# A fixed order for the first eight token tiles of a fused linear-attention and gated-MLP kernel

## The chip, the cores and the metric

The kernel runs on one core of one Trainium2 chip. A core has five engines that run their own instruction queues and meet only through semaphores: TensorE (PE, matrix products; PEld is its weight load), VectorE (DVE), ScalarE (ACT), GpSimd (POOL) and SyncE (SP), which here only issues DMA transfers. Sixteen DMA engines move data between HBM and the on-chip memory (SBUF). TensorE writes to PSUM, eight banks of 128 x 512 floats.

The metric is the device time of one execution in microseconds (us). A verdict compares the changed kernel with the kernel before on the same chip.

## The reference

```python
xn = layernorm(x)                              # x: 1 x 2048 x 1024, no gain or bias, eps 1e-5
q, k, v = heads(xn @ wqkv)                     # 32 heads of 32
phi(u)  = [softmax(u @ w_phi), softmax(-u @ w_phi)]
kv, z   = phi(k)^T v, sum over tokens of phi(k)
s = merge(phi(q) kv / (phi(q) z + 1e-6)) @ wo
h = sigmoid(xn @ w_gate) * (xn @ w_up)         # 1024 -> 3584
out = x + s * silu(h @ w_down)
```

All in 32-bit floats.

## The kernel before, in words

The 2048 tokens are two chunks of 1024, a chunk is eight tiles of 128 tokens. The large products (V, K and Q projections, gate and up, down, output) are each done as seven products of half-size blocks instead of eight (a Strassen-like scheme). The seven operand pairs are called B11, T2, T3, B21, T1, T4 and B22. Each operand needs sums of input blocks on the activation side and sums of weight blocks on the weight side. A float32 product is made of three matmuls of a reduced 32-bit type: `split` writes a high part (ScalarE cast, L124) and a low part (VectorE subtraction, L125), and `mm3` (L127 to L131) multiplies high by high, high by low and low by high into one bank.

The opening of chunk 0 is what concerns us. For each of its eight tiles: the tile is loaded (L151), VectorE takes mean and variance (L161, L162), a chain of nine small operations makes scale and shift (L166 to L175, on GpSimd for chunk 0, with one square root on ScalarE and one reciprocal on VectorE), ScalarE normalizes the tile in place (L177), TensorE transposes it in two halves of four blocks (L193), and ScalarE copies the halves out of PSUM (L197). Tiles 0 to 3 give the blocks B11 and B21, which are also split straight from PSUM; tiles 4 to 7 give B12 and B22. With the matching tile of the first four they form the sums T1, T3, T2 and T4 in `x_sums` (L201 to L207): T1 = B12 - B11 on GpSimd, T3 = B22 - B12 on VectorE, T2 = B22 - T1 on VectorE, T4 = B21 - T2 on GpSimd. T3 and T2 overwrite B12 in a ring of two half slots.

Meanwhile the V projection runs: its products in the order B11, B21, T2, T3, T4, T1, B22, each with four groups (one per 128 tokens) of twelve matmuls. Its weight operands are prepared by `prep` (L334), which splits two of four weight rows at a time into a ring of eight slots; the loop calls it as often as slots are free. Four sums of the raw weight blocks of v, two on VectorE and two on GpSimd, are made in `v_sums` (L248 to L255, two halves each) and stored for the second chunk. The K and Q weights are first multiplied with w_phi in `fold`: a load of wqkT, TensorE matmuls with block-diagonal head blocks `bd` (L278), copies (L279), sums on GpSimd (L227 to L230) and stores (L280). The head blocks are filled by GpSimd in `phi_blocks` (L733). A queue called `side` holds the opening's steps; one step is taken after each group of a projection product: tile 1, tiles 2 and 3 with the head blocks, tiles 4 and 5, v's sums, tiles 6 and 7, four K folds, the rest of the operands (`x_rest`), four Q folds.

The order of the instructions on each engine's queue is not that of the program. A planner places them by priority (program order) and by its own timeline of costs, within the data dependencies; `issue_after` and `high_priority` nudge it. Each queue then runs strictly in its order: an instruction that waits holds up all behind it. Before the first tile arrives, TensorE does 28 warm-up transposes of an identity (L719).

Of the kernel before, what the change touches and what calls it, by code (L numbers as in the profile page):

```python
# [48 lines left out]
def hedgehog_glu_kernel(  # L49
# [54 lines left out]
    WARM = 28  # L104
# [43 lines left out]
    last_norm, last_chain = [], []  # L148
# [5 lines left out]
    def norm(tiles, xs):  # L154
        n = len(tiles)
        st = small.tile([P, 2, 2, 6], F32, name=f"bn{tiles[0]}", tag="bn")
        mv = small.tile([P, 2, 2], F32, name=f"mv{tiles[0]}", tag="mv")
        ws = small.tile([P, 4, 2], F32, name=f"lnw{tiles[0]}", tag="lnw")
        for i, xt in enumerate(xs):
            for a in range(2):  # L160
                nc.vector.bn_stats(st[:, i, a], xt[:, a * HB:(a + 1) * HB])  # L161
            nc.vector.bn_aggr(mv[:, :, i], st[:, i])  # L162
        v, r, a, b = [ws[:, q, :n] for q in range(4)]

        eng = nc.gpsimd if tiles[0] < CTT else nc.vector
# [9 lines left out]
        last_chain[:] = [eng.tensor_scalar(b, b, -1.0, None, op0=ALU.mult).ins]  # L175
        for i, xt in enumerate(xs):
            last_norm[:] = [nc.scalar.activation(xt, xt, AF.Identity, bias=b[:, i:i + 1], scale=r[:, i:i + 1]).ins]  # L177
# [9 lines left out]
    def transpose(t, xt, dst):  # L187

        c, th, u = t // CTT, t % CTT // 4, t % 4
        for q in range(2):  # L190
# [6 lines left out]
            nc.scalar.copy(dst[q], tp)  # L197
            if c and i is not None:
                operand(c, i, u, dst[q])

    def x_sums(c, u, first, second):  # L201
        (b11, b21), (b12, b22) = first, second
        t2 = b22 if c else b12
        for i, o, a, b in ((T1, b11, b12, b11), (T3, b12, b22, b12), (T2, t2, b22, b11), (T4, b21, b21, t2)):
            (nc.vector if c == 0 and i in (T2, T3) else nc.gpsimd).tensor_sub(o, a, b)
            if c or i in (T2, T3):
                operand(c, i, u, o)  # L207
# [39 lines left out]

    def v_sums():  # L248
        vec, pool = nc.vector.tensor_tensor, nc.gpsimd.tensor_tensor
        for f, o, a, b, op in ((vec, 3, 2, 3, "add"), (vec, 2, 0, 2, "subtract"),  # L250
                               (pool, 0, 3, 0, "subtract"), (pool, 1, 1, 0, "subtract")):
            for h in range(2):
                f(whole(VA[o] + h), whole(VA[a] + h), whole(VA[b] + h), op=getattr(ALU, op))
# [42 lines left out]
    flow = dict(item=0, made=0, used=0)  # L296
# [36 lines left out]
    def prep():  # L333
        if flow["item"] == len(items):  # L334
            return False
# [168 lines left out]
    def x_task(t):  # L504
        xt = x_load(t, 52)
        norm([t], [xt])
        th, u = t % CTT // 4, t % 4
        transpose(t, xt, halves(53 + th))
# [547 lines left out]
```

## Time and profile before

| what | value |
|---|---|
| median of three runs | 2437.62 us (2436.7 to 2439.03) |
| the profiled execution's own time | 2438.41 us |
| its span, first to last instruction | 2436.6 us |
| TensorE matmul busy | 2389.2 us, 98% |
| VectorE, ScalarE, GpSimd busy | 1717.3, 1006.8, 989.3 us |
| HBM traffic over the span | 245 GB/s |

A row of a group of instructions gives the line, the engine, the operation, what it writes and reads, the shape, how many there are, then the busy time in us with the mean of one in ns, and after the second bar the idle time of the engine just before them with what ended it. A row of the timeline gives start and duration in us. A row of the windows gives for each engine the busy time and in brackets the number of instructions, then the clock granted to TensorE (1.00 is full), the share of time that the DMA engines were busy, and what they moved in GB/s. A row of the waits gives who waited for whom: us in total, times, the longest. K stands for the K projection, which follows V.

### The profile page before, as it was taken

The numbers are of one execution on the slowest core, as the hardware profiler recorded it, in microseconds if no ns is written. First come the engines' busy times: TensorE is split into PE (matmuls) and PEld (weight loads), VectorE is DVE, ScalarE is ACT, GpSimd is POOL, SyncE is SP. The second block draws the span as 40 slices with busy tenths as digits, with TensorE's granted clock in tenths as the row PEclk, the third lists the DMA queues.
The fourth block names the chain that finished last, engine by engine and source line by source line (L and its number), as shares of the span: only waits on it lengthen the run. The fifth ranks groups of instructions, "written<-read, shape, count | busy, mean of one in ns | idle before, by whom it ended". The sixth has DMA issues, their size and how long they took to land.

```text
span 2436.6 us, 32010 instructions
## 1 busy us (share of the span) xinstructions
PE 2389.2 (98%) x11076; PEld 1984.5 (81%) x11076; DVE 1717.3 (70%) x2247; ACT 1006.8 (41%) x1499; POOL 989.3 (41%) x665
## 2 busy tenths in 40 slices
PE   7999999999999999999999999999999999999998
PEld 6788778888888878888888888888888888888887
DVE  6535577778777679747867888646888988855454
ACT  6432344444444344314444444423443334453332
POOL 5540255756656442222353222323333335414554
PEclk8999999999999999999999999999999999999999
DMA  7887787767777787777777666587666666867554
GB/s 275 271 300 248 255 299 259 271 248 268 260 261 249 255 293 249 265 263 250 261 267 272 221 215 224 191 288 247 221 233 238 217 209 229 286 233 251 173 178 147
DMA packets 233234, 599.44 MB, mean 246 GB/s; under 512 B 30576, under 2 KB 30576, under 8 KB 228464
## 3 DMA queue, kind: packets, MB, share of 16 engines
q1 hardware_dynamic: 233072, 597.40, 71.8%
q8 instruction: 87, 1.43, 0.2%
q14 instruction: 75, 0.61, 0.1%
HBM read 361.10 MB, written 236.19 MB: 245 GB/s over the span
## 4 chain that ended last, share of the span: by engine, by line
PE 74%; DMA 7%; DVE 7%; issue 5%; POOL 4%; ACT 2%; SPq 0%; ACTq 0%; POOLq 0%; DVEq 0%
PE bank L129 24%; PE bank L131 24%; PE bank L130 24%; DMA wo_d<-fc 3%; DVE w L125 1%; PE bank L458 1%; DVE x L125 1%; PE bank L630 1%; DVE p L125 1%; DMA fb<-wqkT 1%; DMA fc<-xo_d 1%; PE bank L278 0%; DVE fc L125 0%; DMA out<-fc 0%; DMA fc<-wo 0%
## 5 line engine op out<-in xcount | busy, mean ns | idle before, releaser
L129 PE MATMUL bank<-x,w 128*128 128x512 f32 x2352 | 912.8, 390 | 8.0 <-ACT fb L837 2.3
L130 PE MATMUL bank<-x,w 128*128 128x512 f32 x2352 | 915.7, 389 | 0.0
L131 PE MATMUL bank<-x,w 128*128 128x512 f32 x2352 | 907.1, 389 | 0.0
L129 PEld LDWEIGHTS bank<-x,w 128*128 128x128 f32 x2352 | 441.5, 188 | 102.9 <-ACT fb L837 2.7
L131 PEld LDWEIGHTS bank<-x,w 128*128 128x128 f32 x2352 | 441.6, 188 | 92.0 <-DVE w L125 0.4
L124 ACT CAST w<-fa 128x512 fp32r<-128x512 f32 (+1 forms) x444 | 307.6, 697 | 504.7 <-PE bank L130 371.0
L130 PEld LDWEIGHTS bank<-x,w 128*128 128x128 f32 x2352 | 441.7, 188 | 90.2 <-DVE x L125 0.3
L125 DVE TENSOR_TENSOR w<-fa,w 128x512 fp32r<-128x512 f32 (+1 forms) x444 | 438.5, 992 | 108.7 <-ACT w L124 101.6
L129 PE MATMUL bank<-w,x 128*128 128x512 f32 x708 | 279.5, 395 | 7.8 <-DVE fc L388 3.2
L131 PE MATMUL bank<-w,x 128*128 128x512 f32 x708 | 277.8, 393 | 1.8 <-DVE x L125 1.8
L130 PE MATMUL bank<-w,x 128*128 128x512 f32 x708 | 277.3, 392 | 0.0
L847 POOL TENSOR_TENSOR fb<-fb,fc 128x512 f32<-128x512 f32 x57 | 88.9, 1560 | 243.3 <-DVE fc L846 218.2
L129 PEld LDWEIGHTS bank<-w,x 128*128 128x128 f32 x708 | 133.8, 189 | 38.9 <-DVE fc L388 3.4
L131 PEld LDWEIGHTS bank<-w,x 128*128 128x128 f32 x708 | 133.5, 189 | 29.8 <-DVE x L125 2.5
L130 PEld LDWEIGHTS bank<-w,x 128*128 128x128 f32 x708 | 133.9, 189 | 26.8
L587 POOL TENSOR_TENSOR fc<-fc 128x1024 f32<-128x1024 f32 x32 | 81.5, 2548 | 182.0 <-ACT fc L423 127.5
L846 DVE TENSOR_TENSOR fc<-fc,bank 128x512 f32<-128x512 f32 x84 | 57.4, 684 | 103.7 <-PE bank L131 92.8
L125 DVE TENSOR_TENSOR x<-fa,x 128x512 fp32r<-128x512 f32 x112 | 114.7, 1024 | 18.0 <-ACT x L124 17.9
L125 DVE TENSOR_TENSOR w<-fb,w 128x512 fp32r<-128x512 f32 (+1 forms) x114 | 102.4, 899 | 32.8 <-ACT w L124 31.1
L124 ACT CAST w<-fb 128x512 fp32r<-128x512 f32 (+1 forms) x114 | 71.3, 626 | 118.7 <-PE bank L130 97.0
L599 POOL TENSOR_TENSOR fc<-fc,sa 128x1024 f32<-128x1024 f32 x32 | 70.4, 2199 | 101.1 <-DVE sa L596 101.1
L847 POOL TENSOR_TENSOR fc<-fc 128x512 f32<-128x512 f32 x27 | 43.4, 1608 | 134.8 <-DVE fc L846 106.9
(246 smaller groups left out, 3281.1 us busy)
## 6 DMA issues: line engine op xcount, KB each, us to landing
ws_d<-w SPq DMA_DIRECT2D x112, 512.0 KB, 4.2
w<-ws_d SPq DMA_DIRECT2D x112, 512.0 KB, 5.0
fa<-w_gu SPq DMA_DIRECT2D x84, 512.0 KB, 4.2
fa<-h_d SPq DMA_DIRECT2D x84, 512.0 KB, 4.3
fa<-wf_d SPq DMA_DIRECT2D x32, 1024.0 KB, 6.3
h_d<-fc SPq DMA_DIRECT2D x120, 256.0 KB, 3.6
fc<-e_d SPq DMA_DIRECT2D x48, 512.0 KB, 3.7
fc<-qkv_d SPq DMA_DIRECT2D x80, 256.0 KB, 4.7
```

The lines of the kernel that those rows point to most:

```text
L124: nc.scalar.copy(o[0], src)
L125: return nc.vector.tensor_sub(o[1], src, o[0].bitcast(F32))
L129: nc.tensor.matmul(o, a[0], b[0], start=first, stop=False, **kw)
L130: nc.tensor.matmul(o, a[0], b[1], start=False, stop=False, **kw)
L131: nc.tensor.matmul(o, a[1], b[0], start=False, stop=last, **kw)
L458: nc.tensor.matmul(kvb[g // 2][:, g % 2 * 256:g % 2 * 256 + 256], v[:, g].rearrange("p a f -> p (a f)"), ph[:, g].rearrange("p a f -> p (a ...
L587: nc.gpsimd.tensor_mul(ez, e, zb)
L599: nc.gpsimd.tensor_mul(e3, e3, r2[:, :, None].to_broadcast([P, 32, DH]))
L630: nc.tensor.transpose(ps[:, j * P:(j + 1) * P], e[:, k * P:(k + 1) * P], ident)
L846: v = nc.vector.tensor_add(b, u2 if q == 3 else u1, bank)
L847: nc.gpsimd.tensor_mul(g, g, b)
```

## The change

The eight tiles of chunk 0 get an order written out by hand. A context manager `in_order` adds, for all instructions traced inside it, an order without a wait between each one and the one traced before it on the same engine. The opening becomes a generator `tiles()` of nine steps; each step is traced in order on VectorE, ScalarE and GpSimd. The first step runs before the V loop, the others from `side`. From the start until after the fourth group of the first product, TensorE's instructions are ordered too.

Besides: 36 warm-up transposes instead of 28; tile 1 is loaded before v's first weight block, which is loaded in two halves; the scale chain of tiles 0 to 3 runs on VectorE (tiles 2 and 3 share one), that of tiles 4 to 7 stays on GpSimd; the copies of tiles 0 to 3 out of PSUM are put off and done two at a time (`keep_two`); `prep` is held to one weight item per `made()` until the ninth step; T2 is now made as T3 + B11, T3 and T2 are written to slots of their own, B12 gets four half slots; T1 and T4 follow on GpSimd at the end; three of v's four weight sums are on VectorE and they come in the sixth step; the head blocks are filled in the fifth. The loads of tiles 6 and 7 and v's last two weight blocks stand in the first and second steps. The K folds start four steps of `side` later than before.

```diff
-    WARM = 28
+    WARM = 36
...
+    @contextmanager
+    def in_order(*engines):
+        traced = nc.cur_bb.bb.instructions
+        last = traced[-1]
+        yield
+        start = next(k for k in reversed(range(len(traced))) if traced[k] is last) + 1
+        for i in traced[start:]:
+            if i.engine in engines:
+                if i.engine in queued:
+                    tc.add_manual_dep(i, queued[i.engine].name,
+                                      mybir.DependencyInfo(mybir.DependencyClass.NoSync, mybir.DependencyReason.DATA),
+                                      reason="in_order")
+                queued[i.engine] = i
...
-        eng = nc.gpsimd if tiles[0] < CTT else nc.vector
+    def scales(tiles, mv, eng=nc.vector):
...
-    def transpose(t, xt, dst):
+    def transpose(t, xt, dst, kept=None):
...
                 operand(c, i, u, tp)
-            nc.scalar.copy(dst[q], tp)
+                kept.append((dst[q], tp))
+            else:
+                nc.scalar.copy(dst[q], tp)
...
+            yield
...
     def v_sums():
...
+        v_sum(nc.vector, 3, 2, 3, "add")
+        v_sum(nc.vector, 2, 0, 2, "subtract")
+        v_sum(nc.vector, 0, 3, 0, "subtract")
+        v_sum(nc.gpsimd, 1, 1, 0, "subtract")
...
-        if flow["item"] == len(items):
+        if flow["item"] == min(len(items), flow["until"]):
             return False
...
-    b12s, b22s = Ring(halves(10)), halves(8, 9)
+    b12s, b22s = halves(10, 26), halves(8, 9)
+    t3s, t2s = halves(52, 53), halves(27, 24)
...
-    v_load(0)
-    xts += [x_load(t, XS[t]) for t in range(1, 4)]
+    xts.append(x_load(1, XS[1]))
+    for h in range(2):
+        nc.sync.dma_start(slots[39 + h], v_block(0, 0)[:, 2 * h:2 * h + 2])
+    xts += [x_load(t, XS[t]) for t in range(2, 4)]
...
+    def t32(u):
+        nc.vector.tensor_sub(t3s[u], b22s[u], b12s[u])
+        nc.vector.tensor_add(t2s[u], t3s[u], first[u][0])
+        operand(0, T2, u, t2s[u])
+
+    def t14():
+        for u in range(4):
+            (b11, b21), b12 = first[u], b12s[u]
+            nc.gpsimd.tensor_sub(b11, b12, b11)
+            nc.gpsimd.tensor_sub(b21, b21, t2s[u])
+
+    def tiles():
+        for n in range(WARM):
+            nc.tensor.transpose(banks[3][:, n % 4 * P:(n % 4 + 1) * P], ident, ident)
+        mv0, take = stats((0,))
+        take(0, xts[0])
+        normalized(xts[0], *scales((0,), mv0))
+        mv1, take = stats((1,))
+        take(0, xts[1])
+        rb = scales((1,), mv1)
+        parts = transpose(0, xts[0], first[0], kept)
+        made()
+        next(parts)
+        made()
+        next(parts)
+        normalized(xts[1], *rb)
+        xts.append(x_load(6, XS[6]))
+        yield
+        parts = transpose(1, xts[1], first[1], kept)
+        mv, take = stats((2, 3))
+        next(parts)
+        take(0, xts[2])
+        keep_two()
+        next(parts)
+        take(1, xts[3])
+        rb = scales((2, 3), mv)
+        normalized(xts[2], *rb, 0)
+        xts.append(x_load(7, XS[7]))
+        v_load(2)
+        v_load(3)
+        yield
+        parts = transpose(2, xts[2], first[2], kept)
+        next(parts)
+        keep_two()
+        next(parts)
+        normalized(xts[3], *rb, 1)
+        mv, take = stats((4, 5))
+        take(0, xts[4])
+        made()
+        yield
+        parts = transpose(3, xts[3], first[3], kept)
+        next(parts)
+        keep_two()
+        next(parts)
+        take(1, xts[5])
+        rb = scales((4, 5), mv, nc.gpsimd)
+        made()
+        normalized(xts[4], *rb, 0)
+        keep_two()
+        yield
+        mv, take = stats((6, 7))
+        take(0, xts[6])
+        second(4)
+        normalized(xts[5], *rb, 1)
+        t32(0)
+        take(1, xts[7])
+        rb = scales((6, 7), mv, nc.gpsimd)
+        phi_blocks()
+        yield
+        second(5)
+        v_sums()
+        normalized(xts[6], *rb, 0)
+        t32(1)
+        yield
+        second(6)
+        normalized(xts[7], *rb, 1)
+        made()
+        t32(2)
+        yield
+        second(7)
+        made()
+        t32(3)
+        yield
+        for u in range(4):
+            operand(0, T3, u, t3s[u])
+            if u % 2:
+                made()
+        t14()
+        flow["until"] = len(items)
+        yield
...
-    todo(x_tiles, 1)
-    todo(lambda: (x_tiles(2, 3), phi_blocks()))
-    todo(x_tiles, 4, 5)
-    todo(v_sums)
-    todo(x_tiles, 6, 7)
+    first_products = in_order(PE)
+    first_products.__enter__()
+    in_turn()
+    for _ in range(3):
+        todo(in_turn)
+    todo(first_products.__exit__, None, None, None)
+    for _ in range(5):
+        todo(in_turn)
```

97 lines of the change are left out of this document (49 added, 48 removed).

## The prediction

> **What bounds the kernel now.** I read the page's engine totals first, then the opening in windows, the waits of TensorE up to 130 us, and the groups and timelines that price single instructions.
>
> ```profile
> PE 2389.2 (98%) x11076; PEld 1984.5 (81%) x11076; DVE 1717.3 (70%) x2247; ACT 1006.8 (41%) x1499; POOL 989.3 (41%) x665
> ```
> TensorE is the bound. The change touches only the part before K's products, so the question is how much TensorE time is lost there, and where. Windows (busy us, instructions in brackets, granted clock, DMA share and GB/s):
> ```profile
> 5.10:8.51 3.41, 1.39 (x13) 1.15 (x11) 1.24 (x4) 0.20 (x1) 1.28 (x7) 1.00 1.04 410
> 18.75:22.17 3.42, 0.76 (x4) 0.30 (x3) 3.28 (x7) 1.34 (x3) 2.04 (x5) 1.00 1.05 387
> 22.17:25.58 3.41, 3.41 (x12) 3.05 (x13) 1.69 (x5) 2.23 (x5) 2.59 (x10) 0.50 1.07 395
> 47.20:59.30 12.10, 7.26 (x38) 6.40 (x36) 8.79 (x10) 10.36 (x18) 4.83 (x4) 0.72 0.34 120
> 59.30:78.00 18.70, 18.70 (x118) 16.68 (x119) 17.23 (x17) 9.75 (x17) 15.47 (x10) 1.00 0.71 220
> 78.00:146.40 68.40, 64.28 (x362) 54.62 (x362) 27.62 (x33) 24.84 (x39) 33.63 (x26) 1.00 0.94 314
> ```
> The hole is at 47 to 59 us; from 59 on TensorE has work, and from 78 the DMA engines are nearly full too (0.94). The waits of TensorE up to 130 us name the holes:
> ```profile
> PE bank L193 <- ACT x L177: 6.2, 2, 3.5
> PE bank L193 <- ACT x L197: 3.6, 1, 3.6
> ```
> Transposes waited twice for normalized tiles (3.5 us for tile 0, the rest for tile 1) and once for a bank (tiles 6 and 7). How much TensorE had done by two instants, in groups up to 34.66 us and then up to 59.2 us:
> ```profile
> L129 PE MATMUL bank<-w,x 128*128 128x512 f32 x16 | 7.9, 496 | 0.4 <-ACT x L124 0.4
> L131 PE MATMUL bank<-w,x 128*128 128x512 f32 x16 | 7.4, 462 | 1.8 <-DVE x L125 1.8
> L130 PE MATMUL bank<-w,x 128*128 128x512 f32 x16 | 7.2, 449 | 0.0
> L193 PE MATMUL bank<-ident,x 128*128 128x128 f32 x32 | 5.8, 350 | 6.2 <-ACT x L177 6.2
> ```
> ```profile
> L129 PE MATMUL bank<-w,x 128*128 128x512 f32 x33 | 14.7, 444 | 0.7 <-ACT x L124 0.7
> L130 PE MATMUL bank<-w,x 128*128 128x512 f32 x33 | 13.8, 419 | 0.0
> L131 PE MATMUL bank<-w,x 128*128 128x512 f32 x32 | 13.5, 426 | 1.8 <-DVE x L125 1.8
> L193 PE MATMUL bank<-ident,x 128*128 128x128 f32 x48 | 9.5, 375 | 9.8 <-ACT x L177 6.2 <-ACT x L197 3.6
> L719 PE MATMUL bank<-ident 128*128 128x128 f32 x28 | 5.0, 361 | 1.5 <-POOL ident masks.py:199 1.5
> L193 PE MATMUL bank<-ident,fc 128*128 128x128 f32 x16 | 1.9, 272 | 0.0
> L278 PE MATMUL bank<-fb 128*128 128x128 f32 x8 | 1.9, 419 | 0.0
> L278 PE MATMUL bank<-fb,x 128*128 128x128 f32 x8 | 1.1, 278 | 0.0
> ```
> So 48 projection matmuls and 32 transposes by 34.66; 98, 64 and 16 fold matmuls by 59.2. At full clock a projection matmul starts every 0.23 us:
> ```profile
> 146.16 0.39 PE L131 MATMUL bank<-w,x 128*128 128x512 f32 x1
> 146.39 0.39 PE L129 MATMUL bank<-w,x 128*128 128x512 f32 x1
> ```
> A transpose or fold matmul is 0.12 (sixteen in 1.9). Work in 47.2 to 59.3 is 16 transposes, 16 folds and two matmuls, 4.1 us: that hole loses 8.0 us.
>
> **The change, part by part.** Prices, from ScalarE's and VectorE's timelines and groups:
> ```profile
> 8.70 1.24 ACT L177 ACTIVATE x<-x,lnw 128x1024 f32<-128x1024 f32 x1 [1.92 <-POOL lnw L175]
> 9.84 1.98 ACT L124 CAST w<-fa 128x1024 fp32r<-128x1024 f32 x2
> 11.72 1.06 ACT L124 CAST x<-bank 128x512 fp32r<-128x512 f32 x2
> ```
> ```profile
> 4.68 1.29 DVE L161 BATCH_NORM_STATS2 bn<-x 128x6 f32<-128x512 f32 x2 [4.68 <-DMA x<-x]
> 6.00 0.21 DVE L162 BATCH_NORM_AGGREGATE mv<-bn 128x2 f32<-128x12 f32 x1
> 6.80 0.16 DVE L168 RECIPROCAL lnw<-lnw 128x1 f32<-128x1 f32 x1 [0.59 <-ACT lnw L167]
> ```
> ```profile
> 379.19 0.16 DVE L171 TENSOR_TENSOR lnw<-lnw 128x1 f32<-128x1 f32 x1
> 379.38 0.15 DVE L172 TENSOR_SCALAR lnw<-lnw 128x1 f32<-128x1 f32 x1
> ```
> ```profile
> L125 DVE TENSOR_TENSOR x<-x,x 128x512 fp32r<-128x512 f32 x8 | 9.1, 1136 | 0.3
> L125 DVE TENSOR_TENSOR w<-fa,w 128x1024 fp32r<-128x1024 f32 x7 | 8.9, 1266 | 4.9 <-ACT w L124 4.7
> L161 DVE BATCH_NORM_STATS2 bn<-x 128x6 f32<-128x512 f32 x12 | 7.7, 679 | 7.6 <-DMA x<-x 7.6
> L125 DVE TENSOR_TENSOR x<-bank,x 128x512 fp32r<-128x512 f32 x8 | 5.3, 683 | 3.0 <-ACT x L124 3.0
> ```
> ```profile
> L253 DVE TENSOR_TENSOR p<-fb,p 128x1024 f32<-128x1024 f32 x2 | 2.4, 1263 | 0.0
> ```
> ```profile
> L253 POOL TENSOR_TENSOR fa<-p,fa 128x1024 f32<-128x1024 f32 x2 | 5.7, 2853 | 2.3 <-DVE fb L253 2.3
> ```
> ```profile
> L733 POOL COPY fb<-fc 32x256 f32<-32x256 f32 x4 | 1.6, 395 | 0.1
> ```
> In short: statistics 1.5 a tile, VectorE's scale chain 1.9 (seven links of 0.2, the square root and two hand-overs), normalizing 1.24, an x split 0.6 then 0.68, a weight split 1.0 then 1.2, a copy like an x cast, a v sum half 1.2.
>
> *To 34.7 us.* Eight more warm-up transposes run where TensorE waits anyway for tile 0: free; without that wait, 1 to 2 us. Tile 0's chain moves from GpSimd to VectorE: 4.7 + 1.5 + 1.9 = 8.1, normalized 9.3, 0.6 earlier. Tile 1 now loads ahead of v's first megabyte (one more DMA issue on SyncE's queue, no more bytes): at 410 GB/s it lands near 6.3. Its statistics and chain end at 11.4; the first weight split is done at 12.6, the x split at 13.3, the second weight split at 14.4, so product B11's first tile ends near 16.7, with six cold matmuls behind that split. Tile 1 is normalized by 14.3 and its transposes follow at once. But then the order blocks: tile 2's statistics stand behind tile 1's first split on VectorE: 16.6 + 0.4 + 0.6 + 0.7 = 18.6, then statistics, split, tile 3's statistics, chain, normalizing: 18.6 + 1.5 + 0.6 + 1.5 + 1.9 + 1.2 = 25.3. TensorE's second tile ends at 21.2, and B21 cannot fill the gap, for TensorE is ordered too until B11's fourth group: 4.1 us idle. Tile 3 follows at 29.7, and B11 ends near 34.7: 48 matmuls, 32 transposes, just what before has by 34.66. The early gain is spent: zero.
>
> *To 46.7 us.* B21's second weight split stands on ScalarE behind the square root of tiles 4 and 5, which waits for tile 5's statistics (35.0): done at 37.9. B21 waits about 2 us; by 46.7 TensorE has 84 matmuls and 48 transposes, before had 96 and 48 by 47.2: 2.7 - 0.5 = 2.2 us behind.
>
> *46.7 to 58.7 us, before's hole.* The head blocks come after GpSimd's chain for tiles 6 and 7 (48.2), four copies of 0.4: folds can start at 50. In reach then: B21's last tile 2.7, tiles 6 and 7 1.8, one and a half K folds (32 matmuls each) 5.4: 9.9 of 12.0. Lost 2.1, and one window of 3.4 us at half clock, 1.7, since an idle stretch cost a half-clock window at 22.17 too. 3.8 against 8.0: 4.2 gained.
>
> *58.7 to 66.6 us, a new hole.* v's sums now stand on VectorE between tile 7's statistics and T2's later operands: 46.4 + 6 x 1.2 = 53.7, with the third sum's 2.4 us taken from GpSimd (5.7 there). Then in fixed order: u = 1's T3 and T2 sums and split to 56.3; T2's first weight split behind normalizing tile 7 to 59.9; u = 2 to 62.6; the second weight split behind tile 7's copies, cast 64.3, done 66.6. T2's first tile starts at 58.7, does six matmuls (1.4) and stops till 66.6; 1.8 of fold is left, since a third fold needs slots that the first one's sums on GpSimd, queued behind v's fourth sum, free only near 68. Lost 7.9 - 3.2 = 4.7. Contention: VectorE operations with both inputs in SBUF averaged 1136 ns against 683 with one in a bank, GpSimd being busy beside them; eight such at +0.45 move the split by 3.6, of which the third fold fills 2.0: +1.6. Bounds: 0, and 8 x 1.0 = 8. One more half-clock window: +1.7 (bounds 0 and 3.4).
>
> The Trainium skill, SBUF — State Buffer, "Who interferes with whom", says that the two engines share a port pair as an exclusive lock: the second one blocks entirely. By it the sum would take the upper bound, 4.4 more, which is a rival below. The quoted mean is a mixture, so the trace bears the lock out only for part of the instructions.
>
> *After that* the work is the same. T2 = T3 + B11 no longer waits for GpSimd's T1, and T3, T2 and B12 have slots of their own: cheaper waits, counted above. The planner puts all unordered work where it likes: 0, bounded by the 4.1 us that TensorE idles from 78 to 146 (68.40 - 64.28), either way. v's four stores of 1 MB move from about 28 to 44 us to 50 to 62, where DMA is 0.34 to 0.71 busy: taken as hidden; uncovered, 4.2 MB at 314 GB/s cost 13 us.
>
> Sum: 0 + 2.2 - 4.2 + 4.7 + 1.6 + 1.7 = +6.0 us. The profiled execution of before took 2438.41 us, 1.8 beside its span of 2436.6, and is 0.8 above the median 2437.62. So 2442.6 span, 2444.4 profiled, 2443.6 as a median.
>
> **Rivals.** *The order closes the hole* (faster). If VectorE's v sums fit its gaps and folds fill every wait, TensorE never starves from 47 on: the 8.0 us go, 2429.6. For it: tile 1 is early, and K folds are 15 us of work that waits for nothing but slots and loads. Against: the two queues above, and DMA at 0.94 behind, which returns what comes early. It decides if T2's second weight split is done before 60. *Every contended operation waits in full:* VectorE and GpSimd two-input work exclude one another, 8 x 1.0 instead of 3.6: 2448.0. *DMA late:* half of v's stores fall beside the folds, 6.5 more: 2450. *The clock stays up:* the idle stretches fall so that neither half-clock window comes, 3.4 less: 2440.2. The Trainium skill, TensorE: Matmul & The Clock Gate, "Part 1", has the clock fall after an idle window of about 3.4 us, which would favour this case; here a window with 0.76 us busy was followed by a half-clock one (the 18.75 and 22.17 rows). *No net change:* unordered work that the planner moves forward covers the new hole: 6.0 - 4.7 = +1.3, 2438.9.
>
> **How the numbers follow.** The order as reckoned 0.34 (0.30 slower, 0.04 same; own range 2440 to 2449), contended in full 0.10 (slower), DMA late 0.08 (slower), hole closed 0.30 (0.28 faster, 0.02 same), clock up 0.06 and no net change 0.12 (same). The 0.2%, 4.9 us, is about what a measurement here can tell from no change. Faster 0.28, same 0.24, slower 0.48. Range 2429 to 2453: the closed hole below, DMA late plus contention above.
>
> **What would show it.** Tile 1's transposes near 16.6; TensorE idle 21 to 25; B21 stopped for a weight split near 38; VectorE in v sums at 46 to 54; T2's first tile stopped near 60 for a weight split; K's first matmul at 152 instead of 146.39. Wrong if TensorE is dense from 47 to 67, or K starts before 146.

## The result, and the profile after

The changed kernel takes 2458.14 us in the median (2453.38 to 2459.57), the kernel before 2437.49 beside it: 1.0083 times as long, with a 95% interval of 1.0071 to 1.0096. That is slower by 20.6 us where 6.0 were forecast, and 5 us above the upper end of the range. The profiled execution took 2458.22 us, with a span of 2456.4.

The engine totals of the profile's page say that TensorE's work is the same but for the eight added warm-up transposes. Its busy time is 6.3 us more and the span 19.8, so most of the loss is time in which it waits:

```profile
PE 2395.5 (98%) x11084; PEld 1987.6 (81%) x11084; DVE 1726.8 (70%) x2270; ACT 1005.3 (41%) x1499; POOL 988.8 (40%) x642
```

Windows of the kernel after (columns: start and end; length, busy us and instructions of TensorE, of its weight loads, of VectorE, ScalarE and GpSimd; granted clock, DMA share, GB/s). The rows answer to those of the prediction; 8.51:11.92, 50.40:64.00 and 182.20:362.40 are added:

```profile
5.10:8.51 3.41, 2.70 (x21) 2.46 (x19) 2.86 (x13) 0.87 (x2) 0.00 (x0) 1.00 0.92 332
8.51:11.92 3.41, 1.59 (x9) 1.04 (x9) 2.86 (x11) 3.03 (x5) 0.00 (x0) 1.00 1.03 416
22.17:25.58 3.41, 0.16 (x1) 0.16 (x2) 1.35 (x9) 1.44 (x2) 0.00 (x0) 1.00 1.06 393
47.20:59.30 12.10, 1.77 (x10) 1.53 (x9) 9.96 (x13) 2.80 (x6) 9.23 (x12) 0.63 0.48 196
50.40:64.00 13.60, 5.32 (x24) 4.95 (x25) 10.04 (x10) 6.28 (x9) 12.97 (x12) 0.50 0.61 251
59.30:78.00 18.70, 16.38 (x91) 14.08 (x90) 14.18 (x10) 10.46 (x18) 18.01 (x10) 0.87 0.78 278
78.00:146.40 68.40, 58.94 (x334) 49.32 (x333) 37.66 (x42) 27.57 (x44) 28.85 (x19) 1.00 0.84 270
182.20:362.40 180.20, 169.94 (x722) 136.54 (x721) 98.22 (x119) 59.22 (x87) 43.01 (x28) 0.98 0.75 260
```

The hole at 47 to 59 us, which the change was to close by 4.2, has become deeper: TensorE is busy for 1.77 us where it had been for 7.26. From 50.4 to 64.0 the clock is at half; TensorE works in 5.32 us of that time. From 78 to 146 TensorE idles 9.5 us instead of 4.1. Between K's third product and the first product of the GLU stage there is the same work (722 matmuls) in 4.8 us more than before, where the same stretch was:

```profile
168.20:343.60 175.40, 166.08 (x722) 134.36 (x721) 97.92 (x121) 60.05 (x88) 43.25 (x30) 1.00 0.77 263
```

The waits of TensorE up to 160 us (releaser; sum, times, longest):

```profile
PE bank L220 <- ACT x L199: 15.7, 3, 10.3
PE bank L310 <- DMA fb<-wqkT: 4.8, 2, 2.9
PE bank L129 <- ACT x L124: 3.9, 5, 1.4
PE bank L310 <- ACT x L311: 3.1, 2, 1.6
```

One wait stands out: 10.3 us for a normalized tile. Behind it are waits of K's folds (L310), for their loads and for their evacuations.

Starts of the first matmul of each product, from TensorE's timelines. Each row shows how far behind the kernel is by then:

| | before, us | after, us | behind, us |
|---|---|---|---|
| 49th projection matmul | 34.7 | 34.6 | 0 |
| T2 | 57.6 | 64.9 | 7.3 |
| T3 | 78.1 | 84.8 | 6.7 |
| T4 | 99.8 | 107.3 | 7.5 |
| T1 | 115.4 | 130.1 | 14.7 |
| K's first product | 146.4 | 156.8 | 10.4 |
| K's third product | 168.2 | 182.2 | 14.0 |
| GLU's first matmul | 343.6 | 362.4 | 18.8 |

K's first product is a flattering mark: after, 32 matmuls of K's folds still stand inside K. K's third product has all folds behind it in both kernels and is the mark used below. So about 7 us are lost before T2, 7 more between T4 and K, and 5 in K and Q.

**Where the 10.3 us come from.** TensorE's timeline (start, duration, line, operation, count; in brackets the idle time ahead and what ended it):

```profile
57.80 1.97 PE L220 MATMUL bank<-ident,x 128*128 128x128 f32 x8 [10.33 <-ACT x L199]
60.65 3.62 PE L310 MATMUL bank<-fb 128*128 128x128 f32 x16 [0.88 <-issue]
```

TensorE waits to transpose tile 6. Tile 6 is normalized late (ScalarE), because GpSimd's chain for tiles 6 and 7 is late (GpSimd), and beside that chain VectorE works on v's sums (VectorE). The fold (L310) stands behind the transposes in TensorE's queue, but it could not have filled the time either: it needs the head blocks, and GpSimd's order puts these (L753) behind the same chain, so that they are done at 58.93 (the run with early folds, below, names that wait):

```profile
56.51 1.24 ACT L199 ACTIVATE x<-x,lnw 128x1024 f32<-128x1024 f32 x1 [6.16 <-POOL lnw L195]
```
```profile
37.42 0.19 POOL L192 TENSOR_SCALAR lnw<-lnw 128x2 f32<-128x2 f32 x1
37.70 1.14 POOL L193 TENSOR_TENSOR lnw<-lnw 128x2 f32<-128x2 f32 x1
38.91 0.19 POOL L194 TENSOR_TENSOR lnw<-mv,lnw 128x2 f32<-128x2 f32 x1
...
49.66 1.11 POOL L190 TENSOR_TENSOR lnw<-lnw 128x2 f32<-128x2 f32 x1 [0.52 <-DVE lnw L188]
50.85 1.06 POOL L191 TENSOR_TENSOR lnw<-lnw 128x2 f32<-128x2 f32 x1
...
55.40 1.07 POOL L195 TENSOR_SCALAR lnw<-lnw 128x2 f32<-128x2 f32 x1
56.42 2.51 POOL L753 COPY fb<-fc 32x256 f32<-32x256 f32 x4
```
```profile
49.50 2.36 DVE L279 TENSOR_TENSOR p<-fb,p 128x1024 f32<-128x1024 f32 x2
51.77 2.35 DVE L279 TENSOR_TENSOR fb<-fa,fb 128x1024 f32<-128x1024 f32 x2
54.04 2.35 DVE L279 TENSOR_TENSOR fa<-p,fa 128x1024 f32<-128x1024 f32 x2
```

A link of two numbers a partition takes 0.19 us on GpSimd. Beside a VectorE sum of 1.2 us with both inputs in SBUF it takes 1.04 to 1.14. The chain for tiles 6 and 7 has six such links, and six half sums run beside it: 6.8 us instead of the 1.6 that the same six take without the sums beside them (the run with VectorE free, below). In the chain for tiles 4 and 5 one link alone is long, the one at 37.70; VectorE's second weight split runs from 37.55 to 38.77.

The Trainium skill, SBUF — State Buffer, "Who interferes with whom", says that the two engines share a port pair as an exclusive lock. The prediction charged it to VectorE's operations. The rows above agree with it and show the other side: each small operation of GpSimd is held up for nearly the whole of one VectorE operation.

### The profile page after: what moved, and what is told of

Same layout as the page of the kernel before. It is cut to its first block, busy times and chain, and to the rows that moved or that the text cites. A ratio compares the mean times of both kernels' runs of the same rounds, so it can differ in the third digit from the quotient of the medians.

```text
span 2456.4 us, 32040 instructions
## 1 busy us (share of the span) xinstructions
PE 2395.5 (98%) x11084; PEld 1987.6 (81%) x11084; DVE 1726.8 (70%) x2270; ACT 1005.3 (41%) x1499; POOL 988.8 (40%) x642
## 5 line engine op out<-in xcount | busy, mean ns | idle before, releaser
L129 PE MATMUL bank<-w,x 128*128 128x512 f32 x708 | 281.2, 398 | 12.6 <-DVE fc L420 5.5
L130 PEld LDWEIGHTS bank<-w,x 128*128 128x128 f32 x708 | 134.9, 191 | 28.0 <-DVE w L125 0.9
L124 ACT CAST w<-fb 128x512 fp32r<-128x512 f32 (+1 forms) x114 | 71.2, 626 | 114.5 <-PE bank L130 92.9
```

The costliest lines, as they stand in the source:

```text
L124: nc.scalar.copy(o[0], src)
L129: nc.tensor.matmul(o, a[0], b[0], start=first, stop=False, **kw)
L130: nc.tensor.matmul(o, a[0], b[1], start=False, stop=False, **kw)
```

## The experiments

All of them compute the whole reference. The edits are to the changed kernel. Times are medians, each with the median of the kernel before from the same chip and its ratio and 95% interval; starts are in us from the beginning of the span, in the one execution of each kernel that was profiled. A table of all of them stands at the end.

### The chain for tiles 6 and 7 on VectorE instead of GpSimd

```
-        rb = scales((6, 7), mv, nc.gpsimd)
+        rb = scales((6, 7), mv)
```

> The changed kernel with one edit: the scale chain of tiles 6 and 7 runs on VectorE instead of GpSimd. Theory A (GpSimd's chain of six small links stretched from 1.7 to 6.7 us beside v's sums on VectorE, so tile 6 came late and TensorE stood 10.3 us in front of its transposes): the chain takes about 2 us, TensorE's wait there falls from 10.3 to about 5 us, K's first matmul comes near 151 to 152 us instead of 156.8, the time is 2451 to 2454. Rival B (VectorE's queue sets T2 anyway, whatever the chain does): T2's product still starts at 64 to 65 and K at 156 or later, 2456 to 2460.

2452.39 us against 2438.81: 1.0063 (1.0048 to 1.0078). The chain takes 1.8 us (48.98 to 50.77) and the wait for tile 6 falls from 10.3 to 4.5. But T2 starts at 68.4, not earlier. The time lies in theory A's range only by luck: K's first product (159.5, where 151 to 152 were expected) and its third (182.3) are no earlier than in the changed kernel, so what this run gains comes later, and where is open. TensorE's timeline of this run, then VectorE's, ScalarE's and GpSimd's:

```profile
52.10 1.97 PE L220 MATMUL bank<-ident,x 128*128 128x128 f32 x8 [4.51 <-ACT x L199]
64.32 3.45 PE L310 MATMUL bank<-fb 128*128 128x128 f32 x16 [10.25 <-issue]
```
```profile
57.50 2.83 DVE L766 TENSOR_TENSOR fc<-x 128x512 f32<-128x512 f32 x1
60.37 2.71 DVE L767 TENSOR_TENSOR x<-fc 128x512 f32<-128x512 f32 x1
```
```profile
63.11 0.62 ACT L124 CAST x<-x 128x512 fp32r<-128x512 f32 x1 [11.07 <-DVE x L767]
63.64 1.07 ACT L226 COPY x<-bank 128x512 f32<-128x512 f32 x2
```
```profile
56.59 5.94 POOL L279 TENSOR_TENSOR fa<-fa 128x1024 f32<-128x1024 f32 x2 [15.44 <-DVE fa L279]
```

The wait has moved. The profile names no releaser for the fold at 64.32, but the fold starts just when the first of two copies on ScalarE (L226, 63.64, 0.53 each) is done, which empty the banks of tile 6's transposes; so the fold waits for a bank, read from the times. In ScalarE's fixed order the copies stand behind a cast for T2 (63.11), which waits for VectorE's T3 and T2 sums (L766, L767). These stand behind v's six half sums, and they take 2.8 and 2.7 us instead of 0.7, as GpSimd's own v sum runs beside them. The head blocks were done at 41.2 in this run, and still no fold filled the 4.5 us: it stands behind tile 6's transposes in TensorE's queue. So GpSimd's chain was the cause of the first wait and not of the loss: another queue behind v's sums was due at nearly the same time.

### v's sums behind T2's sums of the second tile

```
         second(5)
-        v_sums()
         normalized(xts[6], *rb, 0)
         t32(1)
+        v_sums()
```

> The changed kernel with one edit: v's sums stand behind T3, T2 and T2's split of the second token tile on VectorE, not ahead of them. Theory A (contention of the sums with GpSimd's chain): the chain is short, tile 6's transposes come near 53 instead of 57.8, K's first matmul near 152, 2451 to 2454. Rival B (the seven us of sums only change places, T2's weights come after them either way): T2's product starts as late as before, 64 to 66, and the time stays within 2455 to 2460.

2468.34 us against 2438.81: 1.0130 (1.0114 to 1.0147). Neither expectation held: the time is 8 us above the higher of the two. T2 does start earlier (62.1), and so does T4 (103.5). Then T1 starts at 138.0 and K's third product at 193.2, 11 later than in the changed kernel: TensorE waits twice for loads of K's folds (6.1 us, the longer 5.0 at 126.98) and 4.4 us at 134.75 for ScalarE ahead of another fold. v's sums later means v's stores later, and the slots and transfers of K's folds are behind those; that link itself was not measured.

### No fixed order at all

```
-            if i.engine in engines:
+            if False:
```

> The changed kernel with the order left out: the steps are traced as they are, but no instruction is tied to the one before it on its engine. Theory A (the fixed order as such costs the time): K's first matmul within 3 us of before's 146.4, 2437 to 2442. Rival C (what the change does beside the order costs it: K's folds four steps later, weights held back, the sums of v late): K at 152 or later, 2449 or more.

2443.95 us against 2438.81: 1.0026 (1.0013 to 1.0039). All else of the change is still in: the loads, the slots, v's three sums on VectorE, the chains, the split of the steps. So the order as such costs 1.0083 - 1.0026, 14 us of 2438. Its own expectation (theory A, 2437 to 2442) was missed by 2 us: 5 us more than before remain. Up to T4 this kernel is ahead of before (T2 51.0 against 57.6, T4 91.6 against 99.8), and by T1 it is 3.6 behind (119.0 against 115.4). The waits up to 160 us name what took it back:

```profile
PE bank L310 <- DMA fb<-wqkT: 6.3, 3, 5.6
PE bank L220 <- ACT x L199: 3.8, 1, 3.8
```

The folds of K more than the tiles: one waits 5.6 us for its load. Behind such waits the clock is at half for 10.2 us (111.30:121.50, granted clock 0.50), where before has 1.00 throughout 78 to 146. In the change K's folds are traced after all nine steps of the tiles, four steps later than before.

### TensorE's part of the order

```
-    first_products = in_order(PE)
+    first_products = in_order()
```

> The changed kernel with TensorE's order left out and that of the other three engines kept. Theory A (the loss comes from the waits behind the scale chain of tiles 6 and 7, after the part in which TensorE was ordered): the gap of 4 us at 21 us is filled or not, but T2's product still starts at 62 to 65, K at 154 to 157, 2454 to 2459. Rival D (TensorE's fixed order is what costs): K within 4 us of before's, 2438 to 2444.

2460.16 us against 2438.81: 1.0090 (1.0073 to 1.0107), the same as the changed kernel within both intervals; the 10.3 us wait for tile 6 is there too. The order of TensorE costs nothing that can be told; the folds stand behind tile 6 where the planner put them.

### No order, and K's folds traced between the steps

```
-            if i.engine in engines:
+            if False:
...
-    for _ in range(5):
-        todo(in_turn)
+    todo(in_turn)
     for k in range(4):
-        todo(fold, K, k)
+        todo(lambda k=k: (in_turn(), fold(K, k)))
```

> The changed kernel without the order and with K's four folds traced at the same steps as before (beside the steps of tiles 4 to 7 and T3, not after them). Theory C (without the order the opening is 8 us ahead at T4, and the folds, four steps later, give it back at T1): the 8 us are kept, K's third product starts at 160 to 165 instead of 172.0, the time is 2430 to 2436, below before. Rival (DMA at 0.9 in the fold stage returns it whatever the steps): K's third product at 168 to 172, 2438 to 2444.

2433.54 us (12 runs) against 2438.44: 0.9975 (0.9963 to 0.9986). It beats both kernels, before by 5 us. Windows of this run:

```profile
47.20:59.30 12.10, 12.10 (x82) 10.88 (x81) 12.10 (x12) 9.83 (x18) 6.70 (x6) 1.00 0.80 267
59.30:78.00 18.70, 15.62 (x99) 13.04 (x98) 13.15 (x13) 7.18 (x12) 15.27 (x10) 1.00 0.91 290
78.00:146.40 68.40, 68.40 (x369) 58.98 (x368) 29.12 (x33) 26.98 (x41) 34.88 (x24) 1.00 0.90 305
```

This is the closed hole that the prediction had as its first rival, without the order: TensorE is busy throughout 47.2 to 59.3 (11.28 us of it in the run without order above) and again from 78 to 146. K's third product starts at 157.7, 10.5 us ahead of before. Of the 10.5 only a part is left at the end: near the end of the span the same matmul starts 2.6 us earlier than in the kernel before (2405.8 against 2408.4). Where the rest goes is open. Against the run without order above, it is the place of the folds alone that differs: 1.0026 to 0.9975, 12 us.

### K's folds between the steps, with the order

The edit is the second half of the one above.

> The changed kernel, order kept, with K's folds traced at the same steps as before. Theory: the order holds TensorE up to T2 (64.9) with the folds or without, since their banks and head blocks are behind it; what the late folds cost after that (T1 7 us later than T4 was) is won: K's third product at 176 to 179 instead of 182.2, 2450 to 2454. Rival: no effect, 2456 to 2460.

2457.09 us against 2438.44: 1.0078 (1.0065 to 1.0092). Against 1.0083 of the changed kernel this is no gain: the rival held. The longest wait of TensorE is now another:

```profile
PE bank L310 <- POOL fb L753: 11.5, 1, 11.5
```

The fold now stands ahead of tile 6's transposes in TensorE's queue (57.45 and 63.35) and waits as long as they did: for the head blocks (L753), which GpSimd's fixed order puts behind its chain for tiles 6 and 7. The folds' early place is worth 12 us with no order and nothing that can be told with it.

### The chain on VectorE and v's sums a step earlier

```
         take(0, xts[6])
+        v_sums()
         second(4)
...
-        rb = scales((6, 7), mv, nc.gpsimd)
+        rb = scales((6, 7), mv)
...
         second(5)
-        v_sums()
```

> The changed kernel, order kept, with the scale chain of tiles 6 and 7 on VectorE and v's sums moved one step up, into VectorE's idle 4 us ahead of T3's first sum. Theory E (after the chain is freed, TensorE waits at a fold for banks whose copies stand on ScalarE behind a cast that waits for VectorE's T2 behind v's sums): the wait of 10.2 us at the fold goes, T2's product starts at 58 to 61 instead of 68.4, T3's at 77 to 80, the time is 2444 to 2449. Rival (VectorE's sum of work sets it): T2 at 64 or later, T3 at 84, 2451 to 2456.

2454.99 us against 2438.44: 1.0065 (1.0046 to 1.0084). The gain that was expected did not come; the rival's time fits. T2 starts at 63.5, but the profiled execution was the fastest of the four (2446.09), so the starts of this run flatter it. TensorE waits 11.9 us for tile 6 (at 57.88): v's sums now stand ahead of tile 7's statistics on VectorE, and the scale chain of both tiles comes behind those.

### Chain, sums and folds together; and the head blocks early as well

The first has the two edits above together. The second adds:

```
         rb = scales((2, 3), mv)
+        phi_blocks()
...
-        phi_blocks()
```

> The changed kernel, order kept, with the scale chain of tiles 6 and 7 on VectorE, v's sums one step up and K's folds at the steps of before. If the three causes add (about 6 for the chain, 4 to 8 for the sums, 4 to 6 for the folds): K's third product at 166 to 171, 2437 to 2443. If the order itself holds what is left: 2445 or more.

> The run with v's sums a step up, the chain of tiles 6 and 7 on VectorE and K's folds early, and beside these the head blocks filled in the second step, when GpSimd is idle. Theory F (in the run without this edit TensorE stood 7.3 us in front of a fold for the head blocks, which stood behind v's fourth sum on GpSimd): that wait goes, T2's product starts at 63 to 66 instead of 71.2, K's third product at 170 to 173 instead of 177.8, 2442 to 2446. Rival (another wait takes its place, as in the three runs before): T2 at 68 or later, 2447 or more.

2449.36 us against 2438.44, 1.0051 (1.0035 to 1.0067), and 2449.71 against 2437.98, 1.0046 (1.0031 to 1.0061). Three or four mends at once get back some 8 or 9 of the 20 us, and the fourth adds nothing that can be told: theory F's 2442 to 2446 did not come, the time is the rival's. The longest wait, first without and then with the early head blocks:

```profile
PE bank L310 <- POOL fb L753: 7.3, 1, 7.3
```
```profile
PE bank L310 <- ACT x L226: 7.6, 1, 7.6
```

The head blocks were taken out of the way, and the fold now waits as long for a bank whose copies stand in ScalarE's order (as in the first experiment).

### One engine out of the order

ScalarE free, and VectorE free:

```
-        with in_order(DVE, ACT, POOL):
+        with in_order(DVE, POOL):
```
```
-        with in_order(DVE, ACT, POOL):
+        with in_order(ACT, POOL):
```

> The changed kernel with the order kept on VectorE, GpSimd and (first product) TensorE and left out on ScalarE. If ScalarE's queue holds the tile copies back (copies of tile 6 behind a cast that waits for VectorE): T2's product starts at 58 to 61 instead of 64.9, 2450 to 2454. If VectorE's queue, with v's sums in front and GpSimd's chain beside them, sets it: T2 at 63 or later, 2455 to 2460.

> The changed kernel with the order kept on ScalarE, GpSimd and (first product) TensorE and left out on VectorE. If VectorE's order (v's sums held to the sixth step, statistics behind splits) is the cause: the planner makes v's sums by 35 us, GpSimd's chain for tiles 6 and 7 takes 2 us again, T2's product starts at 52 to 57, the time is 2444 to 2450, near that without any order. If not: T2 at 62 or later, 2454 or more.

ScalarE free: 2458.98 us against 2437.98, 1.0087 (1.0073 to 1.0101), and the tile's wait is again 10.3. ScalarE's order alone is not the cause. VectorE free: 2466.31, 1.0118 (1.0104 to 1.0132), slower still. Of its expectation the steps came (the sums by 35 us, the short chain) and the gain did not. The second is of use for the contention. The planner has done v's sums on VectorE by then, and GpSimd's chain for tiles 6 and 7 is short again, in its timeline:

```profile
57.28 0.19 POOL L190 TENSOR_TENSOR lnw<-lnw 128x2 f32<-128x2 f32 x1 [9.13 <-DVE lnw L188]
57.55 0.20 POOL L191 TENSOR_TENSOR lnw<-lnw 128x2 f32<-128x2 f32 x1
```

All six links take 1.6 us: the same instructions, without v's sums beside them. But VectorE did its sums from 24.85 to 33.14, between the links of the scale chain of tiles 2 and 3. TensorE waits 9.1 us for tile 2 (at 36.32), the 49th projection matmul starts at 45.3 instead of 34.6, and that is not made good.

### Where the third sum of v runs

No order, early folds, and the third sum on GpSimd again:

```
-        v_sum(nc.vector, 0, 3, 0, "subtract")
+        v_sum(nc.gpsimd, 0, 3, 0, "subtract")
```

> The fast run without the order and with K's folds at the old steps, and v's third sum back on GpSimd as before. If the third sum on VectorE is part of the gain: GpSimd has 2 x 1.2 us more to do ahead of T2's weights, T2's product comes 1 to 3 us later, 2434 to 2437. If not: T2 within 1 us, 2432 to 2435.

2434.30 us against 2437.98: 0.9982 (0.9970 to 0.9994), within the interval of the same kernel with the sum on VectorE (0.9963 to 0.9986). Which engine has that sum cannot be told from the time where the order is free, though T1 and K's third product start 3.7 and 3.6 us later here. (The expectation's 1.2 us a half is VectorE's price; on GpSimd a half took 2.85 in the kernel before.)

### The order in the first four steps, and in the last five

```
+    turn = [0]
+
     def in_turn():
-        with in_order(DVE, ACT, POOL):
+        turn[0] += 1
+        with in_order(*((DVE, ACT, POOL) if turn[0] <= 4 else ())):
```

The second run has `> 4` there, and TensorE free.

> The changed kernel with the order in the first four steps alone (tiles 0 to 3, with TensorE's order), and steps five to nine left to the planner. Theory G (the loss sits in the second half of the order, where v's sums, GpSimd's chain for tiles 6 and 7 and ScalarE's copies are chained one behind the other): v's sums go to free places, T2's product starts at 51 to 56, the time is 2443 to 2449, near 2444 of the run without any order. Rival H (the first half's late tiles 2 and 3 and B21's late weights set the rest): T2 at 60 or later, 2452 to 2458.

> The changed kernel with the order in steps five to nine alone, steps one to four and TensorE left to the planner. Theory G: tile 6's transposes still wait 8 to 10 us, T2's product starts at 62 to 66, 2453 to 2459. Rival H: T2 at 51 to 57, 2443 to 2449.

First four: 2460.67 us against 2439.42, 1.0082 (1.0065 to 1.0099). Last five: 2449.34, 1.0040 (1.0029 to 1.0051). Against no order (1.0026) the one costs 14 us and the other 3, and the 3 are within the two intervals. In the first, T2 starts at 66.0, as rival H had it, and the time is 3 us above H's range; the loss begins at tile 2, and for another reason than in the changed kernel. VectorE's timeline:

```profile
27.89 2.35 DVE L279 TENSOR_TENSOR fa<-p,fa 128x1024 f32<-128x1024 f32 x2
30.16 0.15 DVE L191 TENSOR_TENSOR lnw<-lnw 128x2 f32<-128x2 f32 x1
```

v's sums are free here, and the planner puts the last of them into the scale chain of tiles 2 and 3, which the order holds together: TensorE waits 10.1 us for tile 2 (at 32.44). In the second run GpSimd's chain for tiles 6 and 7 is stretched again (links of 1.1 us from 43.74 to 50.55, v's sums on VectorE from 43.57 to 50.47), TensorE waits 8.3 us for tile 6, and T2 starts at 59.0. That is the mechanism of the changed kernel, some six microseconds earlier, and it costs less: of theory G's forecast the wait came, T2 and the time did not. So the changed kernel's 14 us cannot be given to one half of its order. The first half alone is as dear as the whole where the planner puts v's sums into a chain that it holds together.

### All runs

| run | ratio to before | T2, us | T4, us | T1, us | K third, us |
|---|---|---|---|---|---|
| before | 1 | 57.6 | 99.8 | 115.4 | 168.2 |
| after | 1.0083 | 64.9 | 107.3 | 130.1 | 182.2 |
| chain on VectorE | 1.0063 | 68.4 | 105.8 | 129.0 | 182.3 |
| sums behind T2's | 1.0130 | 62.1 | 103.5 | 138.0 | 193.2 |
| TensorE free | 1.0090 | 64.2 | 104.0 | 129.1 | 182.1 |
| early folds | 1.0078 | 67.2 | 105.9 | 128.1 | 180.2 |
| chain, early sums | 1.0065 | 63.5 | 103.3 | 124.4 | 176.3 |
| chain, early sums, folds | 1.0051 | 71.2 | 111.1 | 128.0 | 177.8 |
| and early head blocks | 1.0046 | 66.4 | 108.5 | 129.6 | 180.4 |
| ScalarE free | 1.0087 | 66.3 | 112.9 | 130.6 | 182.5 |
| VectorE free | 1.0118 | 64.4 | 116.0 | 134.9 | 188.8 |
| first four steps ordered | 1.0082 | 66.0 | 111.2 | 127.5 | 181.8 |
| last five steps ordered | 1.0040 | 59.0 | 99.8 | 122.0 | 175.9 |
| no order | 1.0026 | 51.0 | 91.6 | 119.0 | 172.0 |
| no order, early folds | 0.9975 | 50.7 | 91.5 | 106.9 | 157.7 |
| the same, third sum on GpSimd | 0.9982 | 51.4 | 91.2 | 110.6 | 161.3 |

## Why the prediction was right or wrong

**The sum against the trace.** What TensorE has done by an instant can be counted, at the prediction's 0.23 us for a projection matmul and 0.12 for a transpose or a fold matmul. By 58.7 us the kernel before has done 98 projection matmuls, 64 transposes and 16 fold matmuls, the changed one 96, 52 and none. By 78 us it is 144, 64 and 88 against 132, 64 and 44. The later marks are those of the table of starts.

| by | behind in the forecast, us | behind as measured, us |
|---|---|---|
| 46.7 us | 2.2 | 0 |
| 58.7 us | -2.0 | 3.8 |
| 78 us | 6.0 | 8.0 |
| K's third product | 6.0 | 14.0 |
| GLU's first matmul | 6.0 | 18.8 |
| the end | 6.0 | 20.6 |

So the sum was nearly right up to 78 us, and that was luck: its three terms were off by -2.2, +8.0 and -3.8 us, which nearly cancel. The largest miss is the last term, the 0 for all that follows, which had been bounded by 4.1 either way and came out at about 12.6. Without it the time would have been near 2446, inside the range.

**To 34.7 us: right in the main.** Tile 1's transposes stood at 16.6 in the forecast, TensorE's idle time at 4.1 us and tile 2 at 25.3, with no net gain by 34.66. Measured, in TensorE's timeline:

```profile
16.79 1.04 PE L220 MATMUL bank<-ident,x 128*128 128x128 f32 x8
...
25.42 1.09 PE L220 MATMUL bank<-ident,x 128*128 128x128 f32 x8 [4.01 <-ACT x L199]
```

Tile 3 came at 31.04 instead of 29.7, and the 49th projection matmul at 34.6 as before. An order that is written out can be walked by hand, link by link; here the walk was within 0.2 us at tiles 1 and 2 and 1.3 us early at tile 3. At tile 2 a slip helped: 16.6 + 0.4 + 0.6 + 0.7 is 18.3 and not 18.6, which would have given 25.0. (Two more slips: the work in before's hole is 4.3 us by the prices given, not 4.1, and "DMA late plus contention" adds up to 2454.5, not 2453. Neither would have brought 2458 into the range.)

**To 46.7 us: 2.2 us behind in the forecast, 0 measured.** The second weight split of B21 ended at 38.77, where the forecast had the stop end near 38. But TensorE's sequence was not what was assumed: the planner had put the first halves of three of B21's groups ahead, which need the first split alone. Groups up to 47.3 us:

```profile
L131 PE MATMUL bank<-w,x 128*128 128x512 f32 x32 | 14.0, 436 | 0.1
L129 PE MATMUL bank<-w,x 128*128 128x512 f32 x32 | 13.8, 446 | 1.4 <-ACT x L124 1.4
L130 PE MATMUL bank<-w,x 128*128 128x512 f32 x32 | 13.5, 423 | 0.6 <-DVE w L125 0.6
```

96 matmuls, as many as before had by 47.2, and no wait for that split: the 0.6 us belong to B11's second split, at 12.23.

**46.7 to 58.7 us: the step that failed first, by 8.0 us.** The forecast gained 4.2 us here. It had GpSimd's chain for tiles 6 and 7 done at 48.2 and folds from 50 on. The chain was done at 56.47, tile 6 was normalized from 56.51, and the head blocks were done at 58.93. Two things were missed. Contention was charged to VectorE's operations and not to GpSimd's small ones, though v's sums were placed by the same walk at 46 to 54, right beside the chain: that is 5.2 of the 8.3 us. (The chain also began late, as tile 7's statistics ended at 48.85 and not at 46.4.) And the folds were to fill the time, while they hang on the head blocks and so on the same chain as the wait that they were to fill. The 9.9 us of work that the sum put into this stretch did not run in it: 1.67 us of TensorE's time in 46.7 to 58.7 were busy, with the 10.33 us wait of the trace in it. That the order as such is worth 14 us is shown, and so is that the hole closes without it when the folds are early (12.10 of 12.10 us busy); that mending this one wait alone would get the 14 us back is shown to be false (the chain on VectorE: 1.0063).

**58.7 to 78 us: 8.0 us lost in the forecast, 4.2 measured, and by another wait.** T2 was to begin at 58.7 and stop for its second weight split, done at 66.6, or 70.2 with contention. T2 began at 64.9, and that split ran from 71.22 to 72.53. But TensorE did not stop for it: the planner had put the first halves of T2's groups and fold matmuls ahead. The one wait between T2's start and 78 us is for a cast of T2's third group, which ScalarE does behind VectorE's sums:

```profile
69.33 0.50 PE L129 MATMUL bank<-w,x 128*128 128x512 f32 x1 [1.44 <-ACT x L124]
```

Contention on VectorE is there and was well sized: six operations from 60.10 to 72.53 took 1.82, 2.08, 1.78, 1.59, 1.00 and 1.31 us instead of 0.69 (1.23 for the two weight splits), 4.4 us more in all where the sum had 3.6. The half clock was priced at 3.4 us in two windows. It came for 13.6 us in one stretch, but as TensorE worked in only 5.32 us of it, it cost about 2.7 (an estimate, half of 5.32). Over the whole opening it is no loss against before: up to 78 us both kernels have 20.5 us at half clock, the kernel before more of it early (8.51:18.75).

**After that, 0: the term that failed by most.** Measured it is about 12.6 us: 6.0 from 78 us to K's third product, 4.8 in K and Q, 1.8 behind them. TensorE waits for K's folds (in its timeline):

```profile
118.71 1.13 PE L310 MATMUL bank<-fb 128*128 128x128 f32 x8 [1.83 <-DMA fb<-wqkT]
...
126.59 1.13 PE L310 MATMUL bank<-fb 128*128 128x128 f32 x8 [2.95 <-DMA fb<-wqkT]
```

The forecast never placed K's folds after the change. They are traced after all nine steps, so their slots and loads come late: the first fold matmul is at 60.7 instead of 54.5, and the load behind the longer wait above was issued at 123.26, 3.3 us before TensorE went on (the loads of this stretch take 4.4 us in the median). Moving the folds is worth 12 us where no order stands in the way. With the order it returned nothing that can be told, so it is not shown that their place alone makes the 6.0 us of the changed kernel. Of the 4.8 us in K and Q 3.9 are busy time, as two stretches of 3.4 us at half clock near 241 and 299 us would make; each comes behind a wait of 2.0 to 2.3 us for VectorE (L420, at 241.25 and 298.22). A third such stretch near 917 us, behind a wait of 1.9 us for the same line, would make most of the last 1.8. The kernel before has none of the three. Why VectorE is late there was not tried.

**The rivals.** *Every contended operation waits in full* had the right mechanism, but charged it to eight VectorE operations (8.0 us; 4.4 measured) and not to the chain on which a tile hung. *DMA late* did not come about in the way it was put: in 59.30:78.00 the DMA engines are 0.78 busy (0.71 before) and in 78.00:146.40 0.84 (0.94 before), so on the mean bandwidth was not short; the loads were issued late. *The order closes the hole* is what the kernel does without the order and with early folds. *The clock stays up* is out: half clock took 13.6 us in one stretch. *No net change* hung on the planner moving work forward into the new hole; the places of TensorE's queue did not suit.

**What stays open.** The order costs 14 us, and no one wait accounts for it. Each mend moved the wait: from the chain to a bank and its copies, to the head blocks, to the copies again. Taking ScalarE or TensorE out changes nothing, taking VectorE out makes it worse. In three of the ordered runs, some 7 us of v's sums on VectorE stand in or beside a scale chain on which a tile hangs (tiles 2 and 3 in two of them, 6 and 7 in the third and in the changed kernel), and the other fixed queues wait behind it; that this is the cause of the 14 us is argued, not shown. A place for the sums that suits the order was not found.

## What to carry to other kernels

Before a chain of tiny operations goes on GpSimd, ask what VectorE does beside it: beside operations with both inputs in SBUF the links cost not their own time but that of the VectorE operation that each meets. Before work is counted as filler for a wait, look what it waits for itself and where it stands in the queue: here the filler hung on the same late chain as the wait that it was to fill. A sum that comes out near the measured time at one mark can do so by errors that cancel, so compare term by term. And an order fixed on several engines at once ties their queues together: removing one wait in it gives the next one, so try the change without the order first; here the same work is 14 us faster without it, and 26 us with its late loads moved as well.

## What the runs showed of the hardware that was not expected

- GpSimd's operations on two numbers a partition take 0.19 to 0.20 us alone and 1.04 to 1.14 beside VectorE's sums or splits with both inputs in SBUF. The sums lost nothing by it (2.36 for two).
- In the other direction two of VectorE's 512-wide sums took 2.83 and 2.71 us instead of 0.7 beside GpSimd's v sum (the first experiment).
- With 36 warm-up transposes TensorE is busy for 2.70 us of 5.10:8.51, and the clock is still full in 8.51:11.92; it falls at 12.8 (1.00 in 8.51:12.80, 0.50 in 12.80:16.20). With 28 it is busy for 1.39, and the clock falls at 8.5. The warm-up transposes that were counted as free go with 4.3 us more at full clock; alone they were not tried. The kernel before:

```profile
8.51:11.92 3.41, 1.93 (x8) 1.57 (x8) 2.04 (x3) 3.23 (x4) 0.15 (x1) 0.50 1.02 408
```

- TensorE need not be idle all the time for the clock to fall. The clock changes at steps of 3.41 us. Cut into such steps, all sixteen traces agree: at full clock, a step with less than 1.49 us busy was always followed by half clock and one with more than 2.0 us never; half clock ended only behind a step with 2.79 us busy or more. A single wait of 2 us can do it: in 238.13:241.54 of the kernel after TensorE is busy for 1.41 us, and 3.4 us at half clock follow.
- With TensorE idle from 47.5 us the half clock came at 50.4, and it stayed until 64.0, though TensorE worked again from 57.8: an idle time of 10 us made 13.6 us at half clock. The Trainium skill, TensorE: Matmul & The Clock Gate, "Part 1", has the clock come back after a busy window of about 3.4 us, and says that the windows run freely; the 6.2 us from 57.8 to 64.0 agree with a wait for a whole busy window.
